# Last-row values of four blocks made early, and eight MLP products put into the slots that this frees

## The chip, the cores and the metric

The kernel runs on one core of one Trainium2 chip. The metric is the device time of one execution in microseconds (us); for the kernel before it is 807.59 us, the median of three runs. Five engines work side by side: TensorE (PE in the profile; PEld are its weight loads), VectorE (DVE), ScalarE (ACT), GpSimd (POOL) and SyncE (SP), which issues nearly all DMA transfers. They order themselves by semaphores. Each engine works off its own list of instructions in order.

## The reference

The input x has 2048 rows of 512. The first half of the computation is attention with a recurrent memory; the second is an MLP. All data are bf16.

```python
h = x + A(layernorm(x))                 # A: attention with memory
out = h + B(layernorm(h))               # B: layernorm again, then the MLP

# A: 64 segments of 32 rows, 8 memory rows, 32 heads of 128
for s in range(64):
    t = concat(mem, xs[s])              # 40 rows
    q, k, v = t @ Wq, t @ Wk, t @ Wv    # 512 -> 32 x 128
    p = softmax(mask(q @ k.T * scale))  # memory rows see all, the others are causal
    o = (p @ v) @ Wo                    # 40 rows of 512
    mem = o[:8]; outs.append(o[8:])

# B: 512 -> 1792 -> 512
y = layernorm(x)
B = gelu(y @ w1 + b1) @ w2 + b2
```

Each segment needs the memory rows that the segment before it made. The rows of x themselves, and so their queries, keys and values, are known from the start.

## The kernel before

**Rows.** A block (`bk`, 16 of them) is 128 rows, that is four segments (`s`; `sg` is its place in the block). Of each segment's 32 rows the first 24 and the 8 memory rows form pack A: 32 rows, the stationary operand `hT`. The last 8 rows of the four segments of a block form pack B: again 32 rows, `hB`. So every product with Wq, Wk or Wv is 32 rows against 4096 columns, done as two passes (`r` = 0, 1). A pass is 16 matmuls in four groups (the `DC` = 4 quarters of 512 input columns); the four matmuls of a group run beside each other as column tiles of 32 columns and 512 streamed columns each (`passes`, line 796). A pass of the same kind that keeps the loaded weights shows up under line 547.

**A segment** (`part`) has six passes of its pack A (K0, K1, Q0, Q1, V0, V1) and two slots, F0 and F1, of a pass's length. Then come scores (SC0, SC1), the products with the values (PVA, PV0, PV1), the output product (WO, line 1083) and the plain scores (SA). The slots hold what the block ahead needs: keys of pack B of block bk+1 in segment 0, its queries in segment 1, its values in segment 2, and the output product of pack B (`wo_B`, line 1112) in segment 3. In block 0 slot F1 of segments 1 to 3 holds 16 filler matmuls (`warm`, line 765), in block 15 the slots of segments 0 to 2 hold the first MLP products of rows 0 to 511 (`w1_first`, line 1233, full 128 x 128 matmuls).

**Pack B's values** go through memory: `v_B_out` copies the passes out of PSUM into `VSB`, `v_B_spread` stores them with four DMAs in `v_last` (line 910) and fetches them with four others into `VBD` (line 916), spread so that each segment of the block finds its rows.

**The opening** (block 0, segment 0) is a list written out, `START`. It begins with the masks and the layernorm of block 0 (`ln1`, lines 734 to 738: statistics and aggregate on DVE, two small steps on POOL, then `xn` on DVE, then four transposes on PE at line 748 and copies on ACT or DVE). Then follow the values of block 0 (B, A), `v_turn` ("Y", line 895), the layernorm of block 1 ("X"), its values, the keys of both blocks, the queries, the first softmax and the first WO, with filler matmuls ("W") between WO's units. ACT's queue loads the two first blocks of x; SP's loads WV, WK, WQ and WO in a fixed order (`chain`), then more blocks of x and the stores and fetches of block 1's values.

**The tail** (`p2_...`). The MLP goes over four stretches of 512 rows (`k`). The weights w1 and w2 (3.7 MB together) are loaded into the space of WK, once attention is done, as four pieces each; a piece waits for the landing of the one two before it. `p2_load` fetches the 512 rows of h, `p2_norm` (line 1184, DVE) normalizes them, `p2_T` (line 1195, SP) transposes them by DMA, `p2_res` (line 1190, POOL) adds b2. `p2_w1` (line 1451) makes one of 14 first products (four matmuls of 128 x 512) and its gelu on ACT (line 1454); `p2_w2` (line 1465) makes the second product of one of the 14 parts for four groups of 128 rows into the four banks of `quad`, four parts behind. At the end of a stretch the last four parts are finished group by group and DVE evacuates each bank (line 1541).

**What sets the order.** PE's order is fixed by `START`, by `ORDERS` for the kinds of segments (`place`: a0 to a3 the first, m0 to m3 the middle by their place in the block, z60 to z63 the last), and by the tail's loops. All other engines' orders come from a planner at build time (`Sched.schedule`): each instruction is put at the earliest gap of its engine by estimated durations and ranks, which `BONUS` shifts by kind and place. It reckons 2.0 us from a DMA to the one that waits for it (`HOP`). `EARLY` puts single steps of the tail into late segments. `align` places up to 8 extra weight loads on a group of a pass (`PADS`), `LEAD` of them in the opening, so that the instruction stream keeps its position against blocks of 256; from segment 4 on it sets that position anew in each block (`LOCK`).

## Time and profile before

| what | value |
|---|---|
| runs of the kernel before | 804.5, 808.98, 807.59 us (median 807.59) |
| profiled execution | span 802.2 us from first to last instruction; the profile gives no other time of it, so 5.4 us of the median lie around it |
| busy share | PE 97%, DVE 75%, ACT 70%, POOL 11% |
| opening, up to the first matmul of segment 1 | 49.0 us |
| attention, segments 1 to 63 | 49.0 to about 702.5 us |
| tail: last parts of attention and rows 0 to 511 | to 725.9 us |
| rows 512 to 1023, 1024 to 1535, 1536 to 2047 | from 725.9, 750.3, 774.6 us to the end |

The span is cut by what PE does; a stage is read from the rows of PE in that stretch: where a row has an idle time in brackets, PE waited, and the name behind it is what it waited for. Busy shares over the span mix the opening, where the weights come in, with the middle, where PE has hardly a gap. A row's length is the time from its first matmul's start to its last one's end; since matmuls overlap, the distance between the starts of two rows tells more.

### The profile page before, as it was taken

What the parts mean: (1) busy time and instruction counts of PE and PEld (TensorE: products, weight loads), DVE (VectorE), ACT (ScalarE), POOL (GpSimd) and SP (SyncE); (2) the same over time, 40 slices, a digit from 0 to 9 for tenths busy, and PEclk for the clock granted to TensorE, in tenths of its full rate; (3) what the DMA queues carried; (4) which work ended last, traced back from release to release, by engine and by line L of the source; (5) the groups of instructions that cost most, each with busy time, mean ns of one, the idle gap of its engine ahead of it and who ended that gap; (6) DMA issues with size and microseconds to landing.
All of it is one profiled execution on the core that took longest, in us unless ns stands there. A gap on an engine that the chain in (4) does not pass through costs nothing.

```text
span 802.2 us, 46835 instructions
## 1 busy us (share of the span) xinstructions
PE 775.9 (97%) x21699; PEld 423.1 (53%) x20880; DVE 600.7 (75%) x1847; ACT 558.0 (70%) x1580; POOL 90.1 (11%) x211
## 2 busy tenths in 40 slices
...
DMA packets 65555, 48.77 MB, mean 61 GB/s; under 512 B 28996, under 2 KB 63308, under 8 KB 63820
## 3 DMA queue, kind: packets, MB, share of 16 engines
...
q14 instruction: 33, 0.27, 0.1%
q10 hardware_dynamic: 332, 0.27, 0.1%
...
## 4 chain that ended last, share of the span: by engine, by line
PE 91%; DMA 3%; DVE 2%; ACT 1%; SPq 1%; issue 1%; POOL 0%; DVEq 0%; ACTq 0%
PE ps L796 43%; PE ps L1083 15%; PE ps L547 8%; PE quad L1465 6%; PE ps L1451 5%; DMA WQ<-in_A_Wq_dram 3%; PE ps L1112 3%; PE quad L994 3%; PE quad L1055 2%; PE ps L1025 2%; PE ps L1233 1%; PE ps L963 1%; PE quad L963 1%; SPq L708 1%; PE quad L998 1%
## 5 line engine op out<-in xcount | busy, mean ns | idle before, releaser
L1083 PE MATMUL ps<-WO,OT 128*32 128x256 bf16 x4224 | 140.6, 274 | 0.1
L796 PE MATMUL ps<-WQ,hT 128*32 128x512 bf16 x1864 | 131.6, 379 | 0.7 <-DVE hT L1089 0.5
L796 PE MATMUL ps<-WV,hT 128*32 128x512 bf16 x1364 | 125.2, 381 | 0.0
L796 PE MATMUL ps<-WK,hT 128*32 128x512 bf16 x1700 | 123.6, 380 | 0.1
L815 ACT ACTIVATE kq<-ps 128x512 bf16<-128x512 f32 x160 | 95.4, 597 | 32.3 <-PE ps L796 26.4
L1083 PEld LDWEIGHTS ps<-WO,OT 128*32 128x32 bf16 x4224 | 100.9, 96 | 26.5 <-ACT OT L814 5.5
L814 ACT CAST kq<-ps 128x512 bf16<-128x512 f32 x162 | 94.8, 585 | 19.9 <-PE ps L796 13.1
L814 ACT CAST OT<-quad 128x128 bf16<-128x128 f32 x191 | 84.4, 442 | 27.0 <-PE quad L998 18.8
L839 DVE STREAM_TRANSPOSE KALL<-kq 128x256 f32<-128x256 f32 x160 | 71.2, 445 | 15.0 <-ACT kq L814 11.8
L796 PEld LDWEIGHTS ps<-WQ,hT 128*32 128x32 bf16 x1864 | 50.3, 97 | 58.8 <-issue 19.0
L861 POOL COPY ZC<-QTB 128x256 bf16<-128x256 bf16 x64 | 25.6, 401 | 477.2 <-PE ps L963 455.7
L796 PEld LDWEIGHTS ps<-WK,hT 128*32 128x32 bf16 x1700 | 45.8, 96 | 56.9 <-issue 14.5
L547 PE MATMUL ps<-WV,hT 128*32 128x512 bf16 x684 | 67.6, 379 | 0.0
L796 PEld LDWEIGHTS ps<-WV,hT 128*32 128x32 bf16 x1364 | 38.4, 97 | 47.3 <-issue 36.6
L839 DVE STREAM_TRANSPOSE QT<-kq 128x256 f32<-128x256 f32 x128 | 57.0, 445 | 6.5 <-ACT kq L815 1.9
L1454 ACT ACTIVATE WQ<-ps,b1t 128x512 bf16<-128x512 f32 x42 | 28.9, 688 | 46.6 <-PE ps L1451 46.6
L1095 DVE STREAM_TRANSPOSE TT<-ps 128x256 f32<-128x256 f32 x66 | 29.7, 450 | 36.3 <-PE ps L1083 36.1
L814 ACT CAST VS<-ps 128x512 bf16<-128x512 f32 x65 | 38.1, 586 | 26.6 <-PE ps L796 26.5
L814 DVE CAST VS<-ps 128x512 bf16<-128x512 f32 x63 | 41.8, 663 | 5.4 <-PE ps L796 5.4
L1541 DVE TENSOR_TENSOR WV<-quad,WV 128x512 bf16<-128x512 f32 (+1 forms) x16 | 10.5, 672 | 45.6 <-PE quad L1465 45.6
L982 DVE TENSOR_TENSOR PC<-EC,rsc 128x128 bf16<-128x128 f32 x128 | 39.7, 310 | 4.3
L1112 PE MATMUL ps<-WO,OTB 128*32 128x512 bf16 x512 | 42.1, 381 | 0.4 <-issue 0.2
...
## 6 DMA issues: line engine op xcount, KB each, us to landing
...
```

Of the source, the lines that this page charges most:

```text
L547: return e.add_instruction(mybir.InstMatmult(name="I-%d" % (4000000 + _kept[0]), engine=mybir.EngineType.PE, start_tensor_calc=start, stop ...
L796: ins = e.matmul(o, l, m, start=(k == 0), stop=(k == DC - 1), tile_position=(0, 32 * j), skip_group_check=True)
L814: return {"act": (lambda e: e.copy(out, src), t_act(n, ps_)), "dve": (lambda e: e.tensor_copy(out, src), 0.16 + 1.042e-3 * n * fast)}
L815: return {"act": (lambda e: e.mul(out, src, scale_), t_act(n, ps_)), "dve": (lambda e: e.tensor_scalar(out, src, scale_, None, ALU.mult), ...
L839: S.op("dve", lambda e: e.transpose(out, src), reads=[("kq", i)], writes=[key], dur=t_dve(256) + 0.02, after=after)
L982: S.op("dve", lambda e: e.tensor_tensor(PC[:, r].rearrange("p t a -> p a t"), EC[:, r], bc, ALU.mult), reads=[("EC", r), ("rsc", r)], writ ...
L1083: ins = e.matmul(ps[bank][32 * j:32 * j + 32, 0:256], lhs(slot(h)), wo_cols(h, b), start=(k == 0), stop=(k == 15), tile_position=(0, 32 * ...
L1095: S.op("dve", lambda e: e.transpose(tt.rearrange("p c q t -> p (c q t)"), ps[bank][:, 0:256]), reads=[("ps", bank)], writes=[("TT", par)], ...
L1112: ins = e.matmul(ps[bank][32 * j:32 * j + 32, :], OTB[:, bk % 2, slot(h), :], WO[:, h, :], start=(k == 0), stop=(k == 7), tile_position=(0 ...
L1451: ins = e.matmul(ps[bank][:, 0:SBT], W1[:, cc, fc * P:(fc + 1) * P], hnT_of(k)[:, cc, :], start=(cc == 0), stop=(cc == DC - 1))
L1454: S.op("act", lambda e: e.activation(gT[:, fc, :], ps[bank][:, 0:SBT], ACTF.Gelu_apprx_tanh, bias=b1t[:, fc:fc + 1], scale=1.0), reads=[(" ...
L1465: S.op("pe", lambda e: e.matmul(quad[:, t, :], lhs, W2[:, fc, :], **flags), reads=[("W2", part_of(fc))] + gT_keys(k, fc), writes=[("ps", t ...
```

## The change

Three things are moved or added, and a few small ones go with them.

1. **Opening.** A fifth small load on ACT's queue brings the last 8 rows of each of the 16 segments of blocks 11 to 14 (128 rows) into `xr` slot 6. A new step "A" in `START` (`ln_ahead`) normalizes them (`norm1`, in the buffers of index 0 that block 0 and block 2 use), transposes them with four matmuls on PE, and copies the result into `xT` (128 x 512), and the part of block 14 from there into `hB` slot 4 on POOL. Right behind it come the values of pack B of blocks 11, 12 and 13: six passes, ahead of the first keys. Their results are kept in `hnT0` (11, 12) and in one half of `OTB` (13), and are stored in `v_last` by twelve DMAs at the end of the chain on SP.
2. **Segments 1 and 2.** Slot F1 holds a pass of block 14's values each, in place of the 16 filler matmuls; they go through `VSB` to `v_last`.
3. **Segment 2 of blocks 10 to 13.** The slots F0 and F1, which held the values of blocks 11 to 14, now hold one first MLP product each of rows 512 to 1023 (`w1_mid`): 8 of 14 over the four blocks. They run as column tiles (`w1_tiles`: 16 matmuls of 32 columns by 512). The raw sums are copied to `kq` and stored in a new buffer `g_mid`. The rows come from `h_mid` by four loads, normalizations and DMA transposes in segments 34 to 39 (`hx`, `hn` 4 to 7 in `EARLY`), the weights by four loads into `VSB` in segments 41, 44, 48 and 52. The fetch of the stored values into `VBD` stays in segment 2.
4. **Tail.** Two loads of 512 KB bring the sums back into `gT`, behind the last piece of w2; ACT makes eight gelus from them; rows 512 to 1023 make 6 first products in place of 14. Their `p2_res` no longer waits for block 15's statistics.
5. **Small ones.** The same steps for rows 0 to 511 move from segments 51 to 55 to segments 54 to 58. `w1_first` in block 15 runs as column tiles too. An instruction that only reads a PSUM bank after another read on the same engine no longer waits for that one (`o.free`). The statistics of the second layernorm add 1.00001 and 1e-10 in place of 1e-5, in the same instruction. `LEAD` is 255 in place of 199, one bonus changes its sign, the loads of rows from 1024 on get a bonus of -15 (`hxk`), and the changed segments get their own name (g2) with the order and bonuses of m2.

```diff
-LATE, RAW, LEAD = 0, 12, 199
+LATE, RAW, LEAD = 0, 12, 255
+AHEAD = (11, 12, 13, 14)
...
-EARLY = {51: (("hx", 0, 0.2),), 52: (("hn", 0, 0.2), ("hx", 1, 0.6)), 53: (("hn", 1, 0.2), ("hx", 2, 0.6)), 54: (("hn", 2, 0.2), ("hx", 3, 0.6)),
-         55: (("hn", 3, 0.2),), 57: (("w1", 0, 0.6),), 58: (("w1", 6, 0.2),), 59: (("w1", 1, 0.1),), 61: (("w1", 2, 0.39),),
+EARLY = {34: (("hx", 4, 0.2),), 35: (("hn", 4, 0.2), ("hx", 5, 0.6)), 36: (("hn", 5, 0.2), ("hx", 6, 0.6)), 37: (("hn", 6, 0.1),),
+         38: (("hx", 7, 0.6),), 39: (("hn", 7, 0.2),), 41: (("w1m", 0, 0.1),), 44: (("w1m", 1, 0.1),), 48: (("w1m", 2, 0.1),), 52: (("w1m", 3, 0.1),),
+         54: (("hx", 0, 0.6),), 55: (("hn", 0, 0.2), ("hx", 1, 0.6)), 56: (("hn", 1, 0.2), ("hx", 2, 0.6)), 57: (("hn", 2, 0.2), ("hx", 3, 0.6), ("w1", 0, 0.6)),
+         58: (("hn", 3, 0.2), ("w1", 6, 0.2)), 59: (("w1", 1, 0.1),), 61: (("w1", 2, 0.39),),
...
-START = (("B", "V", 0, (0, 6), (1, 7)), "V", "Y", "X", ("B", "V", 1, (0, 6), (1, 7)), ("B", "K", 0, (0, 4), (1, 6)), "K0", "K1", ("B", "K", 1, (0, 4), (1, 6)),
+START = (("B", "V", 0, (0, 6), (1, 7)), "V", "Y", "X", ("B", "V", 1, (0, 6), (1, 7)), "A", *(("B", "V", b, (0, 6), (1, 7)) for b in AHEAD[:3]), ("B", "K", 0, (0, 4), (1, 6)), "K0", "K1", ("B", "K", 1, (0, 4), (1, 6)),
...
-                if p.eng == E and E not in self.self_sync:
+                if p.eng == E and (E not in self.self_sync or p in o.free):
...
+        last_rows = A_x[0].rearrange("(g t) d -> g t d", t=SEG)[4 * AHEAD[0]:4 * AHEAD[0] + 16, NA:SEG, :]
+        first(lambda e: e.dma_start(xr[:, 6, :], last_rows), 128, [("xr", 6)])
...
+        def ln_ahead():
+            norm1(0, xr[:, 6, :], ("xr", 6))
+            pb = qbf(128)
+
+            def tr(e):
+                for cc in range(DC):
+                    ins = e.transpose(pb[:, cc, :], xn[:, 0, cc * P:(cc + 1) * P], ident[:])
+                return ins
+            S.op("pe", tr, reads=[("xn", 0), "ident"], writes=QK, dur=0.25, mode=MF, ni=8)
+            S.either(copy2(xT[:], pb, 512), reads=QK, writes=["xT"])
+            S.op("pool", lambda e: e.tensor_copy(hB[:, 4], xT[:, :, 3 * SEG:]), reads=["xT"], writes=[("hB", 4)], dur=0.3)
...
+        def w1_mid(fc, bank):
+            r = fc % 2
+            for cc in range(DC):
+                w1_tiles(bank, W1M[:, cc, r * P:(r + 1) * P], cc, VSB_KEYS)
+            g = kq[:, 4 + r].rearrange("p a e b -> p (a e b)")
+            S.named(S.either(copy2(g, ps[bank][:, 0:SBT], 512), reads=[("ps", bank)], writes=[("kq", 4 + r)]), "gm%d" % r)
+            S.dma(lambda e: e.dma_start(gd[:, fc, :], g), 128, reads=[("kq", 4 + r)], writes=[("gd", fc)])
+
+        def w1_tiles(bank, w, cc, keys):
+
+            def f(e):
+                for j in range(4):
+                    ins = e.matmul(ps[bank][32 * j:32 * j + 32, :], w[:, 32 * j:32 * j + 32], hnT0[:, cc, :], start=(cc == 0), stop=(cc == DC - 1),
+                                   tile_position=(0, 32 * j), skip_group_check=True)
+                return ins
+            S.op("pe", f, reads=keys + [("hnT", "first", t) for t in range(TBS)], writes=[("ps", bank)], dur=.2142, mode=MC, ni=8)
...
-                if bk == 0 and r == 1:
+                if r == 1 and s in (1, 2):
+                    v_B(AHEAD[3], s - 1, bank_of["F1"])
+                elif bk == 0 and r == 1:
                     warm(bank_of["F1"], 4)
...
-                if sg == 2 and 0 < bk < NTB - 1:
+                if sg == 2 and bk + 1 in AHEAD:
+                    w1_mid(2 * AHEAD.index(bk + 1) + r, bank_of["F%d" % r])
+                    if r == 1:
+                        v_B_fetch(bk + 1)
+                elif sg == 2 and 0 < bk < NTB - 1:
                     v_B(bk + 1, r, bank_of["F%d" % r], back["F%d" % r])
...
-                chain += spread["out", 1] + spread["in", 1]
+                chain += spread["out", 1] + spread["in", 1] + [w for b in AHEAD[:3] for w in spread["out", b]]
...
+        NM = 2 * len(AHEAD)
+        for i in range(2):
+            c = slice(i * NM // 2, (i + 1) * NM // 2)
+            S.named(S.dma(lambda e, c=c: e.dma_start(gT[:, c, :], gd[:, c, :]), 64 * NM, reads=[("gd", fc) for fc in range(NM)[c]], writes=[("gT", fc) for fc in range(NM)[c]],
+                    after=used["WQ"] + gate + pieces[-1:]), "gm")
...
+        for fc in range(NM):
+            S.named(S.op("act", lambda e, fc=fc: e.activation(gT[:, fc, :], gT[:, fc, :], ACTF.Gelu_apprx_tanh, bias=b1t[:, fc:fc + 1], scale=1.0),
+                         reads=["b1t"], writes=[("gT", fc)], after=gelus[:1], dur=0.66), "gl")
...
-                p2_w1(k, fc)
+                if k != 1 or fc >= NM:
+                    p2_w1(k, fc)
```

97 lines of the change are left out of this document (66 added, 31 removed), and 5 rows, old and new, of tables (BONUS, ORDERS).

## The prediction, made before the result was known

> **What bounds the kernel now.** I read the page first (engine shares, chain), then PE's waits by stretch, then the opening and the tail in order of time on each engine.
>
> ```profile
> span 802.2 us, 46835 instructions
> PE 775.9 (97%) x21699; PEld 423.1 (53%) x20880; DVE 600.7 (75%) x1847; ACT 558.0 (70%) x1580; POOL 90.1 (11%) x211
> PE 91%; DMA 3%; DVE 2%; ACT 1%; SPq 1%; issue 1%; POOL 0%; DVEq 0%; ACTq 0%
> ```
>
> TensorE is busy 97% and holds 91% of the chain that ended last; DMA holds 3%, one wait in the opening. PE's waits between 60 and 700 us (who waited for whom, total, times, longest):
>
> ```profile
> PE quad L1055 <- issue: 0.7, 1, 0.7
> PE ps L796 <- DVE hT L1089: 0.5, 2, 0.3
> ```
>
> So the middle, blocks 1 to 15, is a stream of matmuls without gaps: there an edit counts by the matmuls it adds or takes away. The opening does have gaps (PE in order of time; columns: start, length, engine, line, operation, count, idle before and its releaser):
>
> ```profile
> 25.71 0.40 PE L748 MATMUL quad<-ident,xn 128*128 128x128 bf16 x4 [0.74 <-ACT VBD L814]
> 26.50 1.92 PE L796 MATMUL ps<-WV,hB 128*32 128x512 bf16 x32 [0.39 <-ACT hB L814]
> 28.24 1.91 PE L796 MATMUL ps<-WK,hB 128*32 128x512 bf16 x32
> ...
> 31.73 1.91 PE L796 MATMUL ps<-WK,hB 128*32 128x512 bf16 x32
> 33.47 0.82 PE L796 MATMUL ps<-WQ,hB 128*32 128x512 bf16 x12
> 35.34 0.40 PE L796 MATMUL ps<-WQ,hB 128*32 128x512 bf16 x4 [1.05 <-DMA WQ<-in_A_Wq_dram]
> ...
> 39.55 0.66 PE L963 MATMUL ps<-KALL,ZC 128*32 128x64 bf16 x32 [1.22 <-POOL ZC L861]
> ...
> 41.81 0.26 PE L994 MATMUL quad<-PTC,VS 32*128 32x16 bf16 x16 [0.74 <-DVE rsc L979]
> ```
>
> The reader should see that the keys' passes at 28.24 begin without a wait, although WQ is still on its way. The only wait between the new work and the queries is 1.05 us for WQ's last quarter. The chain names the same load:
>
> ```profile
> 7.24 28.05 DMA WQ<-in_A_Wq_dram
> ```
>
> The gaps at 39.55 and 41.81 are latencies of the first softmax and follow the queries wherever these go.
>
> **The opening: six passes and a transpose.** PE's order is the written list START, so A and the passes of blocks 11, 12 and 13 stand between block 1's values (26.50) and the first keys (28.24). A pair of passes takes 28.24 - 26.50 = 1.74 us; three pairs take 5.22 us. A itself is four transposes, a copy of 512 columns, then PE, which has nothing else in its order. Before, from transposes to the first matmul took 26.50 - 25.71 = 0.79 us with a copy of 128 columns in it:
>
> ```profile
> 26.15 0.27 ACT L814 COPY hB<-quad 128x128 bf16<-128x128 bf16 x1 [0.49 <-PE quad L748]
> 26.45 0.48 ACT L814 COPY hT<-quad 128x384 bf16<-128x384 bf16 x1
> ```
>
> By 128 and 384 columns (0.27 and 0.48 us) 512 take 0.58, so A costs 0.79 + 0.31 = 1.10 us (bounds 0.8, the short copy's, and 1.5). Evacuation of the passes hides in the next pass on the other bank. The extra padding (LEAD 199 to 255: 56 weight loads) I take at nothing, because block 1's pair already carries 8 extra loads to a group and takes the 1.74 us of the unpadded pair at 31.73. This row shows those loads, 96 beside 30 matmuls (columns: stretch, length, busy and count on PE, PEld, DVE, ACT, POOL, clock, DMA share, GB/s):
>
> ```profile
> 26.00:28.00 2.00, 1.61 (x30) 1.13 (x96) 0.00 (x0) 1.12 (x3) 0.00 (x0) 1.00 1.01 422
> ```
>
> Then the new 128 KB load, third of its kind on ACT's queue. DVE's part of the opening:
>
> ```profile
> 9.88 0.69 DVE L734 BATCH_NORM_STATS2 stt<-xr 128x6 f32<-128x512 bf16 x1 [6.82 <-DMA xr<-in_A_x_dram]
> ...
> 12.75 0.69 DVE L734 BATCH_NORM_STATS2 stt<-xr 128x6 f32<-128x512 bf16 x1 [1.97 <-DMA xr<-in_A_x_dram]
> 13.48 0.18 DVE L735 BATCH_NORM_AGGREGATE agg<-stt 128x2 f32<-128x6 f32 x1
> 14.04 1.79 DVE L694 MEMSET KALL<- 128x2080 uint32 x1 [0.38 <-issue]
> 15.75 0.23 DVE L738 TENSOR_SCALAR xn<-xr,agg,rst 128x512 bf16<-128x512 bf16 x1
> ```
>
> The two loads landed 2.87 us apart, so the third should land at about 12.75 + 2.87 = 15.62. The planner gives a load two microseconds, so it will very likely put the new statistics right behind block 1's, ahead of xn (15.75), which PE's first values wait for (the new aggregate comes behind xn, which reads the same slot). DVE runs in order: statistics at 15.62 to 16.31. If the memset moves behind xn, xn is 0.6 us late; if it stays ahead of it, with its 0.38 of issue, xn starts when 16.7 + 1.79 is over, 2.7 us late. Bounds 0 and 2.7; I take the middle of the two, 1.6. Formerly 1.05 us of such a delay would have vanished in the wait for WQ; with 6 us more ahead of it PE comes too late to wait at all. Opening: 5.22 + 1.10 + 1.6 - 1.05 = **+6.9 us**.
>
> TensorE's clock fell after the softmax gaps:
>
> ```profile
> 42.00:46.00 4.00, 3.56 (x113) 2.40 (x102) 1.98 (x6) 1.74 (x7) 0.00 (x0) 0.57 1.10 349
> ```
>
> A mean of 0.57 over 4 us is 1.7 us lost. The gaps stay, only later; I take no change, with bounds of -1.7 (not lost) and +1.7 (lost twice). The Trainium skill ("TensorE: Matmul & The Clock Gate", Part 1) has a free-running window of about 3.4 us decide this, so that a shift may place the gaps otherwise; by it either bound is open, and no sum here hangs on that.
>
> **Segments 1 and 2.** Block 14's passes take the place of 16 filler matmuls each, of the same shape: nothing on PE. One copy of 512 columns per segment (0.58 us as above) is new on ACT or DVE; it lies beside PE's weight products, and without that cover it would cost up to 1.2 us in all. The twelve stores of 64 KB follow block 1's fetches on SP, and block 14's four come in segment 2; behind them stand block 2's and 3's transposes, whose rows PE first needs in segments 4 and 8.
>
> **The middle.** In segment 2 of blocks 10 to 13 (s = 42, 46, 50, 54) two passes of 16 column tiles become two MLP products of 16 column tiles, with the same 512 streamed columns: nothing. DVE gains four normalizations, SP four loads, four transposes, four weight loads and eight stores. The slowest kind to land is
>
> ```profile
> hnT<-xn SPq DMA_TRANSPOSE x4, 4.3
> ```
>
> and the last of these is issued in segment 39 for a product in segment 42; without that cover PE would stand in the slot, and the segment's weight products behind it, by what the landing lacks. The reads of a PSUM bank after another read lose their wait for the same engine; what this may give PE is bounded by PE's listed waits, or, more widely, by 5.5 us of weight loads waiting for OT:
>
> ```profile
> L1083 PEld LDWEIGHTS ps<-WO,OT 128*32 128x32 bf16 x4224 | 100.9, 96 | 26.5 <-ACT OT L814 5.5
> ```
>
> I take nothing: the copy these loads wait for is the first reader of its bank and had no such wait.
>
> In block 15 six products change from full matmuls to column tiles. Block 10's slot against block 15's:
>
> ```profile
> 482.42 1.06 PE L796 MATMUL ps<-WV,hB 128*32 128x512 bf16 x16
> 483.32 0.40 PE L796 MATMUL ps<-WK,hT 128*32 128x512 bf16 x4
> ...
> 668.41 1.04 PE L1233 MATMUL ps<-hnT,hT 128*128 128x512 bf16 x4
> 669.37 0.40 PE L796 MATMUL ps<-WK,hT 128*32 128x512 bf16 x4
> ```
>
> 0.90 us against 0.96: six times 0.06 gives **-0.4 us**. The Trainium skill ("TensorEngine Tiling (Array Packing)", Key Properties) says that changing the tiling mode drains the array, which agrees.
>
> **The tail.** Rows 512 to 1023 lose 8 products:
>
> ```profile
> 725.93 4.66 PE L1451 MATMUL ps<-WQ,WK 128*128 128x512 bf16 x20
> ...
> 731.29 1.03 PE L1451 MATMUL ps<-WQ,WK 128*128 128x512 bf16 x4
> 732.15 1.03 PE L1465 MATMUL quad<-WK,WQ 128*128 128x512 bf16 x4
> ...
> 750.28 4.66 PE L1451 MATMUL ps<-WQ,WK 128*128 128x512 bf16 x20
> ```
>
> One takes 732.15 - 731.29 = 0.86 us, eight **-6.9 us** of a stage that PE fills from 725.93 to 750.28. The five products at 725.93 also covered the evacuation of rows 0 to 511; now second products follow at once and need the four banks back. DVE:
>
> ```profile
> 723.61 0.69 DVE L1541 TENSOR_TENSOR WV<-quad,WV 128x512 bf16<-128x512 f32 x1 [2.79 <-PE quad L1465]
> 727.70 1.38 DVE L1184 TENSOR_SCALAR WV<-WQ,agg,rst 128x512 bf16<-128x512 bf16 x4 [3.40 <-DMA WQ<-h_mid]
> 729.00 1.88 DVE L1541 TENSOR_TENSOR WV<-quad,WV 128x512 bf16<-128x512 f32 x3
> ...
> 750.55 0.69 DVE L1541 TENSOR_TENSOR WV<-quad,WV 128x512 bf16<-128x512 f32 x1 [0.17 <-PE quad L1465]
> ```
>
> Undisturbed (750.55) the last evacuation ends 0.96 us after PE's last matmul; the three second products ahead of its bank take 0.65. **+0.4 us** with the signal. The eight gelus, 8 x 0.69 = 5.5 us, fit into ACT's idle stretch:
>
> ```profile
> 726.99 0.69 ACT L1454 ACTIVATE WQ<-ps,b1t 128x512 bf16<-128x512 f32 x1 [6.89 <-PE ps L1451]
> ```
>
> If the sums landed late, each gelu would hold PE up to 0.69 us. SP issues these two loads of 512 KB after a wait for W2's last piece; queued behind them are W1's pieces and the transposes of rows 512 to 1023:
>
> ```profile
> 717.57 5.66 SPq L1195 DMA_TRANSPOSE WQ<-WV  x4
> 723.39 0.45 SPq L1178 DMA_DIRECT2D WQ<-h_mid  x1
> ```
>
> These transposes ended at 723.23, some 2.7 us before PE used them; now they are due after 16 second products, 3.5 us later. W1's first two pieces are first used by rows 1024 to 1535. I take +0 (bounds 0 and 2).
>
> **Sum:** 6.9 - 0.4 - 6.9 + 0.4 = **0.0 us** on a span of 802.2. The runs of before have a median of 807.59 (804.5 to 808.98), 5.4 us above the span; what lies around it isn't touched. Forecast: **807.6 us**, no change that a measurement of this kernel can tell (it tells about 0.5%, 4 us).
>
> **Rivals.** (1) *The evacuation stays behind the next rows' normalization.* In the profile DVE's second to fourth evacuation stood behind four normalizations that waited for a load; the fourth ended at 730.88. PE would want that bank at 725.93 + 0.65 = 726.58: 4.3 us of stall, 811.9 us, and later still by what SP's two new loads hold up the load in question (up to 2 us). It decides from the point where the normalization's place in DVE's order is ahead of the second evacuation. For it: that is the order seen. Against: the load now has a bonus of -15 instead of -6.38, and the evacuations have become more urgent by four products. Chance 0.20, slower. (2) *The new statistics delay nothing* (they land or stand behind xn): -1.6 us, 806.0, still no change. Chance 0.17. (3) *Dropped self-waits pull ACT's copies forward everywhere*: up to the 5.5 us above, 802.1, faster. For it: DVE and ACT are 75% and 70% busy, so that chains bind somewhere. Against: PE's listed waits in the middle are below 2 us. Chance 0.13.
>
> **How the numbers follow.** The forecast with its own bounds (opening -1.6 to +1.1, clock 1.7 either way) has 0.50 and lies at 804.3 to 810.4. The range reaches towards both outer rivals, 803 to 813: (3) in full lies just below it, and (1) with a full 2.7 us of delay in the opening just above. Faster by over 0.5%: (3) and the clock kept with (2), 0.18. Slower: (1) and the upper edge of the forecast, 0.20. The rest, 0.62, is no change.
>
> **What would show it.** Right: first queries (formerly 35.34) without a wait for WQ and 6 to 8 us later at the segment's end; xn after 16.3; a stretch of 17.5 to 18 us for rows 512 to 1023 where 24.35 stood; 0.90 us for block 15's slots. Wrong: keys that begin before 33 us, a PE gap over 1 us at the turn to rows 512 to 1023, or another time per block between segments 4 and 59.

## The result, and the profile after

The changed kernel takes 815.82 us (median of six runs, 810.48 to 817.59), the kernel before 807.32 (six runs, 804.5 to 808.98). The ratio is 1.0107, with a 95% interval of 1.0083 to 1.0131: it is slower by about 1%, and the time lies above the range of the forecast. The profiled execution took 813.48 us, with a span of 811.7, 9.5 us more than before. The page of the changed kernel, engine shares and chain:

```profile
span 811.7 us, 47209 instructions
PE 776.5 (96%) x21830; PEld 425.5 (52%) x21072; DVE 603.1 (74%) x1849; ACT 556.2 (69%) x1594; POOL 88.5 (11%) x214
...
q8 instruction: 168, 2.75, 1.5%
...
PE 89%; DVE 5%; ACT 2%; DMA 2%; issue 1%; POOL 0%; ACTq 0%; DVEq 0%
```

PE is as busy as before (775.9 us), but holds 89% of the chain in place of 91%, DVE 5% in place of 2%: PE is waiting. The line on q8, the queue that brings in PE's instructions, is used below. To place the loss, one event per segment serves as a mark: the transposition of WO's result on DVE, the first step of handing the memory on.

| stretch | before | after | difference | forecast |
|---|---|---|---|---|
| start to the first mark (end of segment 0) | 47.97 | 57.95 | +9.98 | +6.9 |
| first to 61st mark (segments 1 to 60) | 620.31 | 624.21 | +3.90 | 0 |
| 61st mark to the end | 133.94 | 129.59 | -4.35 | -6.9 |
| of it rows 512 to 1023 | 24.35 | 19.22 | -5.13 | -6.5 |
| sum | 802.2 | 811.7 | +9.5 | 0.0 |

PE of the changed kernel, in order of time (columns as in the prediction):

```profile
29.59 1.92 PE L835 MATMUL ps<-WV,hB 128*32 128x512 bf16 x32 [0.39 <-ACT hB L853]
31.45 0.40 PE L770 MATMUL quad<-ident,xn 128*128 128x128 bf16 x4
32.74 5.46 PE L835 MATMUL ps<-WV,xT 128*32 128x512 bf16 x94 [0.90 <-ACT xT L853]
39.21 0.39 PE L835 MATMUL ps<-WV,xT 128*32 128x512 bf16 x2 [1.00 <-issue]
...
41.14 1.91 PE L835 MATMUL ps<-WK,hT 128*32 128x512 bf16 x32
...
45.54 1.05 PE L835 MATMUL ps<-WQ,hT 128*32 128x512 bf16 x16
...
49.53 0.66 PE L1019 MATMUL ps<-KALL,ZC 128*32 128x64 bf16 x32 [1.22 <-POOL ZC L906]
...
437.58 0.27 PE L1050 MATMUL quad<-PTC,VS 32*128 32x16 bf16 x16 [0.50 <-DVE PTC L1039]
...
480.98 0.20 PE L1111 MATMUL quad<-PTA,VS 32*128 32x32 bf16 x4 [0.85 <-issue]
...
678.94 1.05 PE L1293 MATMUL ps<-hnT,hT 128*32 128x512 bf16 x16
679.81 0.61 PE L1139 MATMUL ps<-WO,OT 128*32 128x256 bf16 x16
...
740.14 0.59 PE L1546 MATMUL quad<-WK,hT 128*128 128x512 bf16 x2
741.37 0.39 PE L1546 MATMUL quad<-WK,WQ 128*128 128x512 bf16 x1 [0.64 <-DVE WV L1631]
...
743.17 2.98 PE L1546 MATMUL quad<-WK,WQ 128*128 128x512 bf16 x13 [0.21 <-DVE WV L1631]
...
759.79 4.66 PE L1532 MATMUL ps<-WQ,WK 128*128 128x512 bf16 x20
```

**The opening, step by step.** PE comes to the second pair of values at 29.59 where it was 26.50: of these 3.09 us, 2.88 are there from the first transposes on (18.92 against 16.04, both after a wait for xn). A takes 32.74 - 31.45 = 1.29. From 32.74 the six passes last until some 39.4 (two passes of keys at 0.87 end at 41.14), 6.65 us against 5.22 reckoned, and in the middle of them stands a wait of 1.00 us for "issue", that is for nothing the profile knows. The wait for WQ, 1.05 us before, is gone, as the row at 45.54 shows. In sum 2.88 + 0.33 (0.21 up to the second pair and 0.12 in it) + 1.29 + 6.65 - 1.17 (the WQ wait and its latency) = 9.98. DVE, for the opening, one place of the middle (used below) and the tail:

```profile
15.85 0.69 DVE L757 BATCH_NORM_STATS2 stt<-xr 128x6 f32<-128x512 bf16 x1 [2.23 <-DMA xr<-in_A_x_dram]
16.93 1.79 DVE L717 MEMSET KALL<- 128x2080 uint32 x1 [0.38 <-issue]
18.64 0.23 DVE L761 TENSOR_SCALAR xn<-xr,agg,rst 128x512 bf16<-128x512 bf16 x1
...
434.80 0.38 DVE L1186 TENSOR_TENSOR xr<-xr,oN 128x512 bf16<-128x512 bf16 x1
...
435.63 0.25 DVE L1028 TENSOR_REDUCE nmc<-quad 128x2 f32<-128x128 f32 x1
...
437.19 0.24 DVE L1039 STREAM_TRANSPOSE PTC<-PC 128x64 f32<-128x64 f32 x1
...
735.29 4.83 DVE L1230 TENSOR_SCALAR WV<-WQ,agg,rst 128x512 bf16<-128x512 bf16 x4 [9.57 <-DMA WQ<-h_mid]
...
740.65 2.46 DVE L1631 TENSOR_TENSOR WV<-quad,WV 128x512 bf16<-128x512 f32 x4
748.18 1.38 DVE L1230 TENSOR_SCALAR WV<-WQ,agg,rst 128x512 bf16<-128x512 bf16 x4 [5.07 <-DMA WQ<-h_mid]
```

The third load was there at 15.85 (forecast 15.62) and the memset stayed ahead of xn: the case that was priced at 2.7 us, the upper bound, came true: 18.64 against 15.75, 2.9 us. In the tail four normalizations stand ahead of the evacuations of the PSUM banks (740.65), and take 4.83 us in place of 1.38 (748.18). POOL works beside them:

```profile
729.72 4.49 POOL L1236 TENSOR_TENSOR WV<-WQ,b2bc 128x512 f32<-128x512 bf16 x4 [36.59 <-DMA WQ<-h_mid]
735.34 4.64 POOL L1236 TENSOR_TENSOR WV<-WQ,b2bc 128x512 f32<-128x512 bf16 x4 [1.13 <-DMA WQ<-h_mid]
```

DVE's and POOL's blocks run over the same stretch, at 1.2 us a piece each. POOL's four take nearly as long alone (4.49 us at 729.72); it is DVE's that are held up. The Trainium skill ("SBUF — State Buffer", Who interferes with whom) says that an instruction of the tensor_scalar kind can be shut out by a GpSimd instruction that began first, for that instruction's whole length; four of DVE's at the pace of POOL's agree.

DVE's normalizations wait for the load of rows 512 to 1023, the last line of these three of SP:

```profile
724.02 0.49 SPq L1222 DMA_DIRECT2D WQ<-h_mid  x1
728.40 0.81 SPq L1582 DMA_DIRECT2D WQ<-g_mid  x2
729.25 0.43 SPq L1222 DMA_DIRECT2D WQ<-h_mid  x1
```

The two loads of the sums wait for the last piece of W2, until 728.40. The load of the rows, which waits for nothing of the kind, stands behind them. At the turn PE loses (741.37 - 740.57) + 3 x 0.38 = 1.95 us against the undisturbed pace of 0.22 per matmul (740.57 is 740.14 and two of these; the next three matmuls follow 0.60 apart, from 741.37 to 743.17). Middle, 60 to 705 us, who waited for whom:

```profile
PE quad L1050 <- DVE PTC L1039: 1.5, 5, 0.5
PE quad L1111 <- issue: 1.2, 2, 0.8
PE ps L835 <- DVE hT L1145: 0.7, 2, 0.5
...
```

Before, the list had 0.7 us of "issue" and 0.5 us for hT. Two things are new: waits for PTC, the transposed softmax, and more "issue". For the first, the rows of DVE above show one case: a sum for h, 0.38 us at 434.80, which nothing waits for at once, stands ahead of the score maxima (435.63), and PTC, begun at 437.19, lets PE go on at 437.58 only. At the same place of the kernel before, the maxima come straight behind the transposition that precedes this sum.

**What "issue" is.** Laid beside the program, PE's waits for nothing from 0.2 us on all come at the same place, in every kernel here: where the index in PE's own list of instructions, weight loads and semaphore instructions included, is 194 or 195 modulo 256. The 168 packets of q8 carry 2.75 MB, 16 KB each; and PE has 21830 + 21072 instructions by the page, 167.6 times 256. So one packet would bring 256 of them. Below are four such places of the changed kernel, worked out from the packets' times in its trace, together with those of three experiments (PE's gap is from start to start, less the usual 0.22).

```
kernel        PE resumes   packet starts, after   packet   PE resumes,      PE's
              at           the place before       takes    after its end    gap
after         39.21        3.35                   1.09     1.59             1.16
after         480.98       3.18                   1.17     1.52             0.80
after         484.81       1.21                   1.23     1.40             0.25
after         626.44       2.86                   1.00     1.33             0.32
e7_both       47.82        3.07                   1.24     1.45             2.02
e9_best       45.48        3.33                   1.15     1.34             1.61
e11_mid_steps 498.35       3.76                   0.96     1.60             1.47
median of the middle, after  0.89                 1.09     2.09             0
```

PE stands still at these places and goes on 1.2 to 1.6 us after its next packet has landed. Normally the packet starts 0.9 us after PE passes the place before, and 256 instructions last PE 3.5 to 4.9 us in the middle: the slack is 0 to 2 us. Where the packet starts 3 us late, the slack is gone. The Trainium skill ("Runtime: NRT & Kernel Launch", Instruction fetch mechanics) has the list refilled in 16 KB blocks of 256 instructions while the current one runs, and calls the price of crossing "mostly hidden"; the blocks agree, and so does the "mostly" (the median gap is 0), but some crossings cost 0.2 to 2.0 us here.

What makes a packet late isn't shown. Ahead of 39.21 the 16 DMA engines were busy all the time (share 1.06 to 1.13 from 34 to 39 us). Ahead of 480.98 they were nearly idle (0.00 to 0.07 from 475 to 479), and the packet was as late. The late packets of the middle have another thing in common. Over all 13 traces, from 60 to 705 us, 39 of them start more than 2.6 us after the place before. For 38 of these SP issued, between 1.0 us before that place and 0.3 us behind it, a transfer of one of three kinds: the stores of pack B's values in `v_last`, the stores of the sums in `g_mid`, or the loads into `oN`. The same is so for 372 of the 1970 other places. So such a transfer close by goes with a late packet in about one case of eleven, and without one there was hardly any.

Summed over the middle these gaps are 2.42 us before and 3.65 after; in its second half, from 350 us on, 0.52 and 3.24. The sums depend on where a gap is taken to begin, by up to 0.8 us. They are on the low side among small matmuls, which otherwise follow each other much closer than 0.22 (32 of them take 0.37 us at 436.71).

### The profile page after: what moved, and what is told of

Same layout as the page of the kernel before. It is cut to its first block, busy times and chain, and to the rows that moved or that the text cites. A ratio compares the mean times of both kernels' runs of the same rounds, so it can differ in the third digit from the quotient of the medians.

```text
span 811.7 us, 47209 instructions
## 1 busy us (share of the span) xinstructions
PE 776.5 (96%) x21830; PEld 425.5 (52%) x21072; DVE 603.1 (74%) x1849; ACT 556.2 (69%) x1594; POOL 88.5 (11%) x214
## 3 DMA queue, kind: packets, MB, share of 16 engines
q8 instruction: 168, 2.75, 1.5%
## 4 chain that ended last, share of the span: by engine, by line
PE 89%; DVE 5%; ACT 2%; DMA 2%; issue 1%; POOL 0%; ACTq 0%; DVEq 0%
PE ps L835 43%; PE ps L1139 14%; PE ps L557 8%; PE quad L1546 5%; PE ps L1532 4%; PE quad L1050 3%; PE ps L1168 2%; PE quad L1111 2%; PE ps L1081 2%; DMA xr<-in_A_x_dram 2%; PE ps L1293 2%; PE ps L1019 1%; PE quad L1019 1%; DVE TT L1151 1%; DVE hT L1145 1%
## 5 line engine op out<-in xcount | busy, mean ns | idle before, releaser
L853 ACT CAST kq<-ps 128x512 bf16<-128x512 f32 x170 | 99.4, 585 | 25.7 <-PE ps L835 14.3
L835 PEld LDWEIGHTS ps<-WV,hT 128*32 128x32 bf16 x1364 | 39.4, 97 | 46.8 <-issue 36.2
L853 ACT CAST VS<-ps 128x512 bf16<-128x512 f32 x68 | 39.9, 586 | 26.4 <-PE ps L835 26.3
L1535 ACT ACTIVATE WQ<-ps,b1t 128x512 bf16<-128x512 f32 x34 | 23.4, 688 | 42.1 <-PE ps L1532 42.1
L853 DVE CAST VS<-ps 128x512 bf16<-128x512 f32 x60 | 39.8, 663 | 5.1 <-PE ps L835 5.1
L835 PE MATMUL ps<-WQ,hB 128*32 128x512 bf16 x512 | 41.9, 389 | 0.6 <-issue 0.3
L1032 ACT ACTIVATE EC<-ps,nmc 128x64 f32<-128x64 f32 x130 | 39.9, 313 | 1.9 <-DVE nmc L1028 1.6
```

Of the source, the lines that this page charges most:

```text
L835: ins = e.matmul(o, l, m, start=(k == 0), stop=(k == DC - 1), tile_position=(0, 32 * j), skip_group_check=True)
L853: return {"act": (lambda e: e.copy(out, src), t_act(n, ps_)), "dve": (lambda e: e.tensor_copy(out, src), 0.16 + 1.042e-3 * n * fast)}
L1032: ins = e.activation(EC[:, r, sl, :], o[:, 64 * sl:64 * sl + 64], ACTF.Exp, bias=nmc[:, r, sl:sl + 1], accum_out=smc[:, r, sl:sl + 1])
```

## The experiments

Eleven kernels ran. The diffs show the telling lines of each edit. Times are medians; ratios are to the kernel before on the same chip. The two stretches are those of the table above; "gaps" are PE's gaps at the places of 256 in the middle, and the last column is the middle without them.

| kernel | time | ratio (95%) | start to first mark | middle | gaps | middle less gaps |
|---|---|---|---|---|---|---|
| before | 807.32 | 1 | 47.97 | 620.31 | 2.42 | 617.9 |
| after | 815.82 | 1.0107 (1.0083 to 1.0131) | 57.95 | 624.21 | 3.65 | 620.6 |
| e1_stats_behind | 810.13 | 1.0053 (1.0032 to 1.0074) | 54.81 | 625.55 | 5.34 | 620.2 |
| e2_rows_load_first | 812.66 | 1.0088 (1.0056 to 1.012) | 58.54 | 624.91 | 4.92 | 620.0 |
| e3_no_mid_loads | 812.38 | 1.0099 (1.0063 to 1.0135) | 57.79 | 622.51 | 3.91 | 618.6 |
| e4_self_waits | 813.73 | 1.0113 (1.0072 to 1.0154) | 57.32 | 626.24 | 4.82 | 621.4 |
| e5_passes_in_gaps | 810.81 | 1.0036 (1.0014 to 1.0058) | 50.31 | 626.47 | 5.50 | 621.0 |
| e6_turn_order | 814.37 | 1.0078 (1.0047 to 1.0109) | 57.41 | 626.48 | 4.44 | 622.0 |
| e7_both | 808.30 | 1.0005 (0.9985 to 1.0026) | 49.78 | 626.53 | 6.17 | 620.4 |
| e8_before_traffic | 807.39 | 0.9999 (0.9981 to 1.0017) | 48.06 | 621.23 | 3.11 | 618.1 |
| e9_best | 806.90 | 1.0024 (0.9997 to 1.005) | 50.93 | 623.70 | 3.35 | 620.4 |
| e10_no_padding | 812.33 | 1.0073 (1.0048 to 1.0099) | 54.42 | 627.05 | 6.73 | 620.3 |
| e11_mid_steps | 813.11 | 1.0083 (1.0055 to 1.011) | 55.06 | 626.17 | 5.79 | 620.4 |

The gaps differ by 3 us between kernels with nearly the same middle, and from one execution to the next they come at other places. The middle of one profile is therefore good for some 3 us, and for about 1 us once the gaps are taken out.

**e1: the new statistics behind block 1's xn.**

```diff
-            norm1(0, xr[:, 6, :], ("xr", 6))
+            norm1(0, xr[:, 6, :], ("xr", 6), [S.last_writer[("xn", 1)]])
```

> Edit: the changed kernel, with the statistics of the new 128 rows ordered behind the second normalization (xn) of the first two blocks; everything else stays. Theory A (the new statistics, standing ahead of the first normalizations on DVE, hold up xn and with it PE's first products): xn's second write back from 18.64 to about 15.8 us, PE's first transposes from 18.92 to about 16.0, the first query product of segment 1 from 58.88 to 56.0 and the time 2.9 us shorter (profiled execution 813.5 to about 810.6). Rival B (the new load itself takes the rings from the weights and rows, whatever DVE's order): the transposes stay after 18 us and the time changes by less than 0.5 us. Both theories: the six passes still take 5.2 us plus their own stall.

Measured: the first mark at 54.81, 3.1 us earlier; ratio 1.0053 against 1.0107, with intervals that don't overlap. DVE of e1:

```profile
14.41 1.79 DVE L717 MEMSET KALL<- 128x2080 uint32 x1 [0.38 <-issue]
16.12 0.23 DVE L761 TENSOR_SCALAR xn<-xr,agg,rst 128x512 bf16<-128x512 bf16 x1
```

The memset begins 2.5 us sooner and xn with it (16.12; 15.75 before). So it is the place of the new statistics in DVE's order, with the load they wait for, that made xn late; the load itself still comes. The mark's other 0.6 us aren't the edit's: up to the second pair of values (25.69 against 29.59) PE gained another 1.4 us, as it did in e11, whose opening is that of after (28.23), and the softmax then lost more clock (0.50 from 48 to 54 us).

**e2: the load of rows 512 to 1023 ahead of the two loads of the sums.**

```diff
-        p2_load(0)
+        hx0 = p2_load(0, hx1)
...
-                    after=used["WQ"] + gate + pieces[-1:]), "gm")
+                    after=used["WQ"] + gate + pieces[-1:], behind=hx0), "gm")
```

> Edit: the changed kernel, with the loads of rows 512-1023 and of rows 0-511 issued on SP ahead of the two loads of the stored sums; everything else stays. Theory A (the stall at the turn comes from rows 512-1023 being loaded behind the sums, which wait for W2's last piece: their normalization then runs on DVE from 735.3 to 740.1 beside POOL's additions and keeps the first evacuation from starting at about 738): the normalization ends before 734, evacuation 1 starts about 738, the 16 second products after the turn take 3.5 to 4.0 us instead of 5.41, time 1.4 to 1.9 us shorter. Rival B (the four evacuations, 0.61 us each, pace PE whatever stands ahead of them, or the bank order does): the 16 products still take over 5 us and the time changes by less than 0.5 us.

Measured: from the 61st mark to PE's end 125.6 us, 1.0 less than after (126.5), where 1.4 to 1.9 were expected; in the time (812.66 us) it can't be told. The evacuations begin at 739.21, in step with PE, and the 0.64 us wait is gone. In its place PE of e2 has

```profile
745.43 1.04 PE L1546 MATMUL quad<-WK,WQ 128*128 128x512 bf16 x4 [0.76 <-DMA WQ<-WV]
```

a wait for the transposed rows, and SP of e2 shows what these stand behind:

```profile
729.84 9.58 SPq L1569 DMA_DIRECT2D WK<-in_B_w_dram  x4
739.46 5.22 SPq L1241 DMA_TRANSPOSE WQ<-WV  x4
```

The third and fourth of W1's pieces wait for the landing of the first two, and hold SP until 739.42. That is the place in SP's order that the prediction named and took at 0 (bounds 0 and 2).

**e6: as e2, with two of W1's pieces ahead of the transposes and two behind them.** It also makes the normalization of rows 1024 to 1535 wait for the last evacuation of rows 0 to 511. In this execution their load landed only after that evacuation anyway (DVE evacuates last at 742.59 and normalizes from 744.91).

```diff
-        for i in range(4):
+        for i in (2, 3):
             piece(W1, w1_d, "W1", i)
...
-                    p2_load(k + 1)
+                    nxt = p2_load(k + 1)
+                    _ = [piece(W1, w1_d, "W1", i, nxt) for i in (0, 1) if k == 1]
```

> Edit: the changed kernel with SP's order at the turn changed: both row loads ahead of the stored sums, then W1's two pieces that rows 512-1023 use, then their transposes, then the row load of the next rows and W1's other two pieces. Theory A (in the run with the row loads first, the transposes, issued behind all four pieces of W1, were what PE waited for, 0.76 us): the transposes issue before 737 us on the changed kernel's scale, no wait over 0.5 us at the turn, the end 2.2 to 2.9 us earlier after segment 60 than in the changed kernel (126.5 us from there to PE's last product, 124 expected). Rival B (the stored sums or W1's pieces then come too late, since the rings are full): a wait for DMA of over 1 us in the first eight activations or at the ninth product.

Measured: 61st mark to PE's end 124.99 us, 1.6 less than after, where 2.2 to 2.9 were expected; 814.37 us. PE of e6 at the turn:

```profile
743.34 2.98 PE L1546 MATMUL quad<-WK,WQ 128*128 128x512 bf16 x13 [0.21 <-DVE WV L1631]
746.16 1.03 PE L1532 MATMUL ps<-WQ,WK 128*128 128x512 bf16 x4
```

The 16 second products run through with one gap of 0.21, and the first ones follow at once. The whole turn now costs the 0.4 us that the prediction gave it. It shows in the trace; in the time, whose interval overlaps that of after, it doesn't.

**e3: the middle without its loads.** Neither rows nor weights are brought in for the eight products: no loads, normalizations or DMA transposes in segments 34 to 39, no weight loads after it. The products run on what lies in the buffers; the stores of the sums stay.

```diff
-EARLY = {34: (("hx", 4, 0.2),), 35: (("hn", 4, 0.2), ("hx", 5, 0.6)), 36: (("hn", 5, 0.2), ("hx", 6, 0.6)), 37: (("hn", 6, 0.1),),
-         38: (("hx", 7, 0.6),), 39: (("hn", 7, 0.2),), 41: (("w1m", 0, 0.1),), 44: (("w1m", 1, 0.1),), 48: (("w1m", 2, 0.1),), 52: (("w1m", 3, 0.1),),
+EARLY = {
```

> Edit: the changed kernel without the steps that serve the products of the middle in segments 34 to 52: four row loads, four normalizations, four transposes and four weight loads are left out, so the eight products of segments 42 to 54 work on what lies in their buffers and the result for rows 512-1023 is not the reference's. PE's work is the same. Theory A (PE's own instruction blocks arrive late in these segments because of this added traffic; the stalls at block boundaries there add up to 2.9 us): the slow segments 33, 36, 37, 39, 40 and 41 (10.6 to 11.4 us) go back to 10.2 to 10.4, segments 1 to 59 take 621 us or a little more instead of 624.2, time 2.5 to 3.5 us shorter. Rival B (the place of the block boundaries or the dropped waits make them, not the traffic): segments 1 to 59 stay at 624 plus or minus 0.7.

Measured: the middle takes 622.51 us, 618.6 without the gaps, against 620.6: some 2 us belong to those steps. From mark 36 to 37 (segment 0 has mark 0) the time comes back from 10.79 to 10.32 (10.22 before); e1, e2 and e4, which keep the steps, have 10.79 to 10.85. From 56 to 57, where the moved steps for rows 0 to 511 run, it stays at 10.67 (10.66 in after, 10.22 before). The list of PE's waits for PTC goes from 1.5 us to 0.8. The gaps do not fall, against the expectation: 3.91 us in place of 3.65. e3 keeps the stores of the sums, and these were issued 0.3 and 0.6 us ahead of the places before two of its late packets (gaps at 498.42 and 540.35). The span is none the shorter (814.5), since in this execution the load of rows 512 to 1023 came a further 1.1 us late. First DVE, then PE, then the clock of e3 (columns of the last: stretch, length, busy and count on PE, PEld, DVE, ACT, POOL, clock, DMA share, GB/s):

```profile
736.40 4.82 DVE L1230 TENSOR_SCALAR WV<-WQ,agg,rst 128x512 bf16<-128x512 bf16 x4 [11.70 <-DMA WQ<-h_mid]
```

```profile
742.47 0.39 PE L1546 MATMUL quad<-WK,WQ 128*128 128x512 bf16 x1 [2.76 <-DVE WV L1631]
...
744.27 4.67 PE L1546 MATMUL quad<-WK,WQ 128*128 128x512 bf16 x13 [0.21 <-DVE WV L1631]
```

```profile
744.00:748.00 4.00, 3.79 (x12) 1.47 (x12) 0.21 (x1) 0.00 (x0) 0.00 (x0) 0.62 0.76 186
```

Here the turn cost 2.76 + 3 x 0.38 us, and on top of it a clock of 0.62 over the next 4 us: 1.5 us more. Whether this place also makes the spread of after's own runs (810.48 to 817.59) wasn't tried.

**e4: the waits for the same engine back.**

```diff
-                if p.eng == E and (E not in self.self_sync or p in o.free):
+                if p.eng == E and E not in self.self_sync:
```

> Edit: the changed kernel with the waits of an engine for its own earlier read of a PSUM bank put back, as they were before the change; order and work stay. Theory A (the middle's loss has nothing to do with these waits): segments 1 to 59 stay at 624 plus or minus 0.7, time within 0.5 us of the changed kernel. Rival B (the dropped waits let copies of ACT and DVE start in another order of events and cost the middle its 4 us): segments 1 to 59 fall to about 620, time 4 us shorter. Rival C (my third rival in the prediction, that dropping them gains up to 5.5 us): time up to 5.5 us longer.

Measured: 813.73 us, ratio 1.0113 against 1.0107; the middle 621.4 less gaps against 620.6, the first mark 57.32 against 57.95. No stretch moves by more than such profiles differ among each other. Rival 3 falls: to within 1 us these waits neither cost before nor gain now.

**e5: e1, and the six new passes in PE's gaps of the first softmax.** A comes between the two passes of block 1's values; block 11's passes and one of block 13's go into the places around Z and the scores, the other one of block 13's and one of block 12's in place of the seven filler matmuls between and behind WO's units, block 12's other one in place of a filler in segment 3; `LEAD` is 199 again.

```diff
-         ("B", "Q", 0, (0, 5)), "Q0", ("B", "Q", 0, (1, 4)), "Q1", "Z", "SC0", "SC1", ("B", "Q", 1, (0, 5)), "PV0", "PV1", "SA", "WO", ("T", "WO", 0, 2),
+         ("B", "V", 11, (0, 7)), ("B", "Q", 0, (0, 5)), "Q0", ("B", "Q", 0, (1, 4)), "Q1", "Z", ("B", "V", 11, (1, 4)), "SC0", "SC1", ("B", "Q", 1, (0, 5)), ("B", "V", 13, (0, 4)), "PV0", "PV1", "SA", "WO", ("T", "WO", 0, 2),
```

> Edit: the changed kernel with the new rows' statistics behind xn (as in the run on the statistics), the new rows' transposes between the two passes of block 1's values, and the six passes of blocks 11 to 13 placed where PE stood idle or did filler work: one before the queries, one in the gap before the first scores, one in the gap before the first weighted values, two in place of the seven fillers at the end, one in place of segment 3's four fillers; opening's padding 199 as in the kernel before. Theory A (the passes cost what they add to PE where nothing is idle; in the gaps they cost nearly nothing): the first transposed output of segment 0 on DVE comes at 49 to 50.5 us (before 47.97, changed kernel 57.95), the time is 7.5 to 9 us shorter than the changed kernel's. Rival B (a pass costs its 0.87 us wherever it stands, since the gaps are waits that start later by as much): that output at 53.5 us or later, 4 to 4.5 us shorter.

Measured: the first mark at 50.31, 4.5 us before e1's and 2.3 behind before's, with five of the six passes made in it; 810.81 us, ratio 1.0036. Of the 2.3 us, 2.05 are one gap for "issue" at 48.35, PE's fourth block. So the passes as such are nearly free where PE has gaps or did filler work; they cost 5.2 us where they were put.

**e7: e5 and e6 together.** The diff is theirs.

> Edit: the passes in the gaps and the turn's order together. By the sum of the two theories 9 to 11 us shorter than the changed kernel: 803 to 808 us where the kernel before has 805 to 807, ratio to it 0.995 to 1.002, with the middle's 3 to 5 us still lost. If the two rivals hold instead: 811 to 813, ratio above 1.005.

Measured: 808.30 us, ratio 1.0005 (0.9985 to 1.0026): the loss is gone, there is no gain. PE of e7 has the same gap as e5, and the clock at that place stays:

```profile
47.82 0.62 PE L1139 MATMUL ps<-WO,OT 128*32 128x256 bf16 x15 [1.96 <-issue]
```

```profile
46.00:48.00 2.00, 0.18 (x8) 0.18 (x11) 1.28 (x4) 0.00 (x0) 0.00 (x0) 1.00 1.05 328
48.00:52.00 4.00, 3.83 (x87) 2.57 (x79) 2.80 (x9) 1.17 (x2) 1.05 (x3) 1.00 0.48 143
```

PE's fourth block came in from 45.1 to 46.4, beside a DMA share of 1.09 (45 to 47 us), that is with all 16 engines busy. PE got from one place of 256 to the next in 5.77 us. Since a packet under that load starts about 3.1 us after the place before, takes 1.24, and PE resumes 1.45 later, 256 instructions can't take PE less than 5.8 us there, however well its gaps are filled. That is an estimate from this one row of the list above, and it takes for granted that the packet starts as late however PE goes.

**e8: the kernel before, with only the traffic of the middle added.** The same loads of rows, DMA transposes, weight loads and stores of sums are issued in about the same segments, into space that is free at that time; nothing uses them, and the computation is that of before.

```diff
+        def mx(i, after): S.dma(lambda e: e.dma_start(hnT0[:, 3, :], hd[:, i, :]), 128, reads=[("hd", i)], writes=["s3"], after=after)
+        def mw(i, after): S.dma(lambda e: e.dma_start(hnT0[:, 1:3, :].rearrange("p c (a f) -> p (c a) f", a=2), w1_d[:, :, 2 * i * P:(2 * i + 2) * P]), 256, writes=["s12"], after=after)
+        def ms(i, after): S.dma(lambda e: e.dma_start(gd[:, i, :], hnT0[:, 3, :]), 128, reads=["s3"], writes=[("gd", i)], after=after)
```

> Edit: the kernel before, with the middle's new transfers alone, which nothing uses: four row loads of 128 KB and four transposes in segments 34 to 39, four weight loads of 256 KB and eight stores of 128 KB in segments 41 to 51; no instruction of PE, DVE or ACT is added. Theory A (transfers delay PE's instruction blocks): the stalls at PE's 256-instruction boundaries between 60 and 705 us, 2.4 us in the kernel before, grow to 3.5 us or more, the new ones in segments 34 to 51, and segments 1 to 59 take 621.3 to 623.5 us instead of 620.3. Rival B (traffic of this size does not matter; the changed order of DVE's and ACT's instructions costs the middle): 620.3 plus or minus 0.7.

Measured: 807.39 us, ratio 0.9999 (0.9981 to 1.0017). The gaps of the second half go from 0.52 to 2.48 us, as they do in after (3.24), while the first half, which is the same program, goes from 1.90 to 0.64. Without gaps the middle is that of before (618.1 and 617.9). PE has no wait for PTC in its list, as before. So the traffic goes with more waiting for instructions in that half, about 2 us, and with nothing else. Summed over the middle the gaps are 3.11, short of the 3.5 expected; in the time, with one profile of each and a first half that moved most of that the other way, nothing is to be seen.

**e10: no padding in the opening.**

```diff
-LATE, RAW, LEAD = 0, 12, 255
+LATE, RAW, LEAD = 0, 12, 0
```

> Edit: the changed kernel without the opening's padding (LEAD 255 to 0), which leaves out 256 weight loads that do nothing, one whole block of PE's instructions; order and work stay. Theory A (the 1.0 us stall at 39.21 us is PE out of instructions: a block of 256 is used up in 6.2 us while the weights fill the rings and the next block starts 3.3 us late): no stall for nothing above 0.3 us before the queries, first transposed output of segment 0 on DVE at 56.8 to 57.2 instead of 57.95 us. Rival B (the stall belongs to the passes' place or a bank): it stays within 0.2 us, at whatever instruction.

Measured: the first mark at 54.42, 3.5 us earlier, three times what was expected; 812.33 us. 0.6 us of it are there by 32.12, where the values of block 11 begin (32.74 in after), and 2.1 by the first scores (47.45 against 49.53). The first 0.6 aren't shown to be the padding's: with the same opening and all its padding, block 11's values begin at 32.04 in e2 and at 31.39 in e11. The 1.5 from there on are its doing: from block 11's values to the scores it takes 15.33 us, and 16.70 to 17.10 in the six profiles with the opening of after, each of which has a gap of 0.9 to 1.3 at the place of 39.21, which doesn't occur in e10. The last 1.4 come from the clock. After, then e10, each by its own time:

```profile
50.00:54.00 4.00, 2.82 (x124) 1.90 (x123) 2.65 (x11) 2.86 (x13) 0.40 (x1) 0.82 0.46 126
53.00:54.00 1.00, 1.00 (x52) 0.94 (x44) 0.54 (x2) 0.48 (x2) 0.00 (x0) 0.50 0.52 144
54.00:58.00 4.00, 4.00 (x88) 2.67 (x84) 2.08 (x7) 1.02 (x2) 0.00 (x0) 0.76 0.33 88
```

```profile
48.00:52.00 4.00, 2.82 (x132) 1.75 (x120) 2.80 (x11) 2.86 (x13) 0.40 (x1) 1.00 0.46 131
52.00:56.00 4.00, 3.90 (x96) 2.61 (x92) 3.26 (x11) 0.94 (x2) 0.00 (x0) 1.00 0.32 83
```

The same work with the same gaps, 2 us sooner, ran at full clock. In after 0.18 x 4 + 0.24 x 4 = 1.7 us are lost. That isn't the padding's doing either: e11, with all of it, has its scores at 48.09, loses no clock (1.00 from 42 to 60 us) and comes to the first mark at 55.06. And e10 leaves out all 255 loads; what the 56 that the change added cost by themselves isn't shown. e10's middle took 2.8 us more than that of after, with 3.1 us more of gaps, so that the span is that of after.

**e11: the new steps of the middle later in their segments.** The fractions that `EARLY` gives say from which point of a segment a step may run; those of the normalizations go from 0.2 to 0.6, and one step of block 7's h gets a bonus of its own.

```diff
-EARLY = {34: (("hx", 4, 0.2),), 35: (("hn", 4, 0.2), ("hx", 5, 0.6)), 36: (("hn", 5, 0.2), ("hx", 6, 0.6)), 37: (("hn", 6, 0.1),),
+EARLY = {34: (("hx", 4, 0.2),), 35: (("hn", 4, 0.6), ("hx", 5, 0.75)), 36: (("hn", 5, 0.6), ("hx", 6, 0.75)), 37: (("hn", 6, 0.6),),
...
-"hxk": -15
+"hxk": -15, "xr7": -40
```

> Edit: the changed kernel with the middle's steps moved within their segments (normalizations from 0.2 to 0.6 of a segment, row loads to 0.75) and block 7's residual addition planned behind the softmax of segment 36; the same transfers and work. Theory A (the even part of the middle's loss is DVE's order: an addition or normalization ahead of the softmax chain that PE waits for): segments 36 and 56 go from 10.79 and 10.66 to 10.22 and 10.3, segments 1 to 59 without the boundary stalls from 620.0-621.4 to 619.0-620.0. Rival B (the even part comes from transfers too): segments 36 and 56 stay above 10.6.

Measured: from mark 36 to 37 it takes 10.21 us in place of 10.79; in after this stretch held PE's wait of 0.50 us at 437.58. From 56 to 57, where 10.3 was expected, it takes 11.27, with a gap of 0.76 in it. PE's waits for PTC go from 1.5 us to 0.5. But the middle in all is 626.17. PE of e11 shows why:

```profile
498.35 0.19 PE L1111 MATMUL quad<-PTA,VS 32*128 32x32 bf16 x2 [1.52 <-issue]
...
500.16 3.13 PE L1139 MATMUL ps<-WO,OT 128*32 128x256 bf16 x56
```

```profile
500.00:504.00 4.00, 4.00 (x114) 3.00 (x114) 0.89 (x3) 1.51 (x4) 0.00 (x0) 0.57 0.56 102
```

A gap of 1.52 us for instructions, and 2 us later the clock falls to 0.57 over 4 us: 1.7 us lost by the clock, 1.4 by the 56 matmuls at 500.16 (the next ones start at 503.06, after 2.9 us, where 1.5 is usual). From mark 42 to 43 it took 13.55 us in place of 10.42. Without the gaps and this loss the middle would be 618.7 to 619.0, an estimate, against before's 617.9.

**e9: everything together.** e7 with `LEAD` 64, e11's steps, and the fetch of the stored values into `VBD` in segment 1 in place of segment 2, where the sums are stored.

> Edit: the run with passes in the gaps and the turn's order, and besides: the opening's padding 199 to 64, the steps of the middle moved within their segments (normalizations at 0.6 of a segment, row loads at 0.75), block 7's residual addition planned behind the softmax of segment 36, and blocks 11 to 14's value fetches a segment earlier than the stores of the products. Theory (DVE's order costs the middle's even part, instruction blocks the rest): segments 36 and 56 go from 10.8 and 10.7 to 10.2 and 10.3, about 1 us; the opening 0.4 us shorter; fewer late instruction blocks in segments 42, 46, 50 and 54, up to 1.5 us; in all 1.5 to 3 us shorter than the kernel with both, ratio to the kernel before 0.996 to 0.999. Rival (the middle's loss is made by chance of where instruction blocks meet transfers, and moving steps only moves it): ratio 1.000 to 1.003.

Measured: 806.90 us, ratio 1.0024 (0.9997 to 1.005); span 802.1. It isn't told apart from before, and has its own gap of 1.61 us at 45.48. The two stretches that the moved steps were to mend come to 10.22 and 10.23 us (marks 36 to 37 and 56 to 57), as expected, and PE's waits for PTC fall to 0.2. But its waits for hT rise from 0.7 to 1.8, and the middle less gaps stays at 620.4. One case: statistics of a block of x, which wait 2.15 us for their load and begin at 413.50, stand ahead of the mark's transposition on DVE (414.33), and PE waits 0.77 us for hT until 415.22. So moving these steps mended one place, and another short chain was held up elsewhere. No version beat the kernel before.

## Why the prediction was wrong, point by point

Four terms failed: xn's delay in the opening was taken at 1.6 us and was 2.9; padding was taken at 0, and without it (e10) 1.5 us less pass; the middle was taken at 0 and lost 3.9; SP's order at the turn was taken at 0 and cost 1.6 more than the 0.4 reckoned there. Each is taken up below.

**What bounds the kernel** held: PE, and each term counted by what it did to PE. But the middle was called a stream without gaps on the strength of a list of waits that has 0.7 us of "issue"; what "issue" was, wasn't asked.

**Six passes, 5.22 us:** right in size (6.65 less the gap of 1.16; 0.27 more went in slower pairs). e5 shows that they needn't have cost it; this is where most of the loss could be had back.

**A, 1.10:** 1.29, within its bounds.

**xn late, 1.6 (bounds 0 to 2.7):** 2.9. This failed: the row showed the memset ahead of xn, with 0.38 of issue, and gave 2.7 if it stayed; the middle of the bounds was taken without a reason that it would move. e1 gives 2.5 of it back. Rival 2 (the statistics delay nothing) is refuted by the same rows.

**The WQ wait, -1.05:** -1.17, right.

**Padding, 0:** failed, as far as e10 can tell: without any of it, 1.5 us less pass between block 11's values and the first scores, most of it the gap at 39.21. What the 56 added loads cost alone stays open. The row that was to show it free (96 weight loads beside 30 matmuls at clock 1.00) was a row of 2 us with 126 instructions, too short to hold a whole block of 256; padding counts into the 256 as matmuls do.

**The clock, 0 (bounds 1.7 either way):** 0 was right: 1.7 us lost before and after. e10 and e11 show that the bound "not lost" was real, at the same work shifted by 2.1 and 1.4 us. That the size came out at 0 was luck. The Trainium skill ("TensorE: Matmul & The Clock Gate", Part 1) has a free-running window of about 3.4 us decide; the low clock was 0.50 (53 to 54 us in after), so that the 1.7 us lost in after and in e11 make 3.4 us each at half speed, which agrees; and 1.96 us of idle in e7 without any fall shows that the length of a gap alone doesn't decide.

**Segments 1 and 2, 0:** right; the first two segments took 10.34 and 10.09 us against 10.66 and 10.09.

**The middle, 0:** failed by 3.9 us, in two ways. Some 2 us (e3: 620.6 to 618.6) come from the new steps by way of the order on DVE: they moved it, so that short work nobody waits for came to stand ahead of a softmax that PE needs at once (434.80). Their transfers alone don't cost this (e8: 618.1 less gaps, no wait for PTC), and with the steps moved the wait goes (e11, e9: 10.21 and 10.22 us from mark 36 to 37). The prediction counted DVE's load (75%) and not its order. The other way is waiting for instructions, 2.7 us more in the second half and 1.5 less in the first, 1.2 in all; the remaining 0.7 isn't placed, but the count of the gaps is on the low side. The first half is the same program in e8 and moved by 1.3 us from one execution to the next, so its part may be chance. In the second half the added transfers are suspected: e8 has them alone and 2.48 us of gaps. Of these the stores of the sums stand out, since e3 has none of the loads and its gaps all the same. No time proves it.

**Block 15, -0.4:** the slot took 679.81 - 678.94 = 0.87 in place of 0.96, as foreseen, and gave nothing: from the first queries of segment 60 to those of segment 63 it took 31.57 us against 31.53 (672.84 to 704.41, 658.85 to 690.38). A wait of 0.2 us for PTC is listed there; where the rest went isn't shown. From there to the end of rows 0 to 511 another 0.6 us went, 0.5 of it in gaps put down to "issue".

**Rows 512 to 1023, -6.9 and +0.4:** the 8 products were worth what was reckoned; the turn cost 1.95 in place of 0.4. The step that failed is the +0 (bounds 0 and 2) for SP's order, the two loads of the sums and what is queued behind them. The load that came late wasn't the next rows' but the stretch's own, behind the sums, and through it the four normalizations stood ahead of the evacuations. That is rival 1's mechanism with another load: its price, 4.3 us, was too high because the normalizations began at 735.29, 5.3 us ahead of the end of PE's last products. e2 and e6 confirm the chain by taking it apart: first the rows, then the transposes. The slack of 2.7 us that the prediction gave these was read from the end of their issue (723.23); in the trace of before the last one landed at 724.42, 1.5 us ahead of its use.

**Rival 3** fell with e4. **The sum:** forecast 0, measured +9.5 in the span: 3.1 from the opening's terms, 3.9 from the middle, 2.5 from the end. No single error explains the miss; those above 0.2 us have one sign, because nearly every unknown cost was taken at nothing or at the middle of its bounds.

**The signs named beforehand:** the queries came without the WQ wait, but 9.98 us later and not 6 to 8; xn at 18.64 (after 16.3); 19.2 us for rows 512 to 1023 (17.5 to 18); 0.87 for the slots; a wait at the turn in four pieces, 1.95 us; and another time per segment in the middle, which had been named as the sign that the prediction is wrong.
